# Nyström attention and a squared-ReLU FFN on one core: token-major A for two batches, landmark sums by adding transfers, and a new order

## The chip, the cores and the metric

The kernel runs on one core of one Trainium2 chip. A core has five engines that each work through their own instructions in order: TensorE (PE for its matmuls, PEld for its weight loads), VectorE (DVE), ScalarE (ACT), GpSimd (POOL) and SyncE (SP). They meet only through semaphores. Transfers are issued by POOL (the software queue, which also casts f32 to bf16 on the way) and by SP (the stores), and are carried out by 16 DMA engines. The metric is the time of one execution on the device in microseconds, as the median of several runs.

## The reference, cut to what matters

Eight batches of eight heads; 576 tokens, 64 columns per head, 32 landmarks per head. Each landmark is the mean of 18 neighbouring tokens. The attention output, laid out as 4608 tokens of 512 columns, goes through a feed-forward network with a squared ReLU.

```python
scale = 1.0 / np.sqrt(D)
q_lm = q.reshape(B, H, m, S // m, D).mean(axis=3)
k_lm = k.reshape(B, H, m, S // m, D).mean(axis=3)
A  = sm(q, k_lm)        # softmax of scale * a @ b^T
Bm = sm(q_lm, k_lm)
C  = sm(q_lm, k)
Z = Bm^T / (norm1(Bm) * norminf(Bm) + 1e-06)
for _ in range(6):
    Z = 2 * Z - Z @ Bm @ Z
attn = A @ Z @ C @ v
x = attn.transpose(0, 2, 1, 3).reshape(B * S, H * D)
h = x @ w_in            # 512 -> 2048
r = np.maximum(h, 0.0)
out = (r * r) @ w_out   # 2048 -> 512
```

## The kernel before

**Who sets the order.** The kernel is written as a list of operations, each with a name, the engines that could do it, a cost on each, what it reads and writes, and the PSUM banks that it takes. A planner (class `Plan`) runs through them once while the kernel is built: at each moment each free engine takes, of its ready operations, the one with the largest tail (the length of work behind it, plus a bias from the table `URGE`); an operation that two engines could do goes to the one that would end first (table `LEAN` shifts that). The result is a fixed order on each engine, emitted as it is. The due times of the planner are its own; on the chip an instruction waits for what it needs, and everything behind it on its engine waits too.

**Stages of one batch b.** Names in the list are those of the operations.

- Loads: `ldk`, `ldq` (L480, two transfers of 590 KB each into tile X), `ldv` (L489, tile V), w_in in eight transfers, w_out in four, all on POOL. At most eight of these transfers are in flight; POOL waits for a free place before it issues the next. Before the change, the order is k and q of batch 0 in turn (k, q, k, q), v of batch 0, k and q of batch 1, w_in, v of batch 1, w_out, and then batch after batch.
- Landmark sums `lm`: PE adds 18 tokens by multiplying X with an identity. Batch 0 is done in two halves. Its first half and the whole of batch 1 are 18 full-array matmuls each (L535, "flat"); its second half and the other batches are 36 matmuls each that use PE as four arrays of 64x64 (L542) and leave two parts in two banks, which `lmc` (two copies) and `lme` (one addition) bring together into LM. The sums are not divided by 18; the scale of the mean is put into the exponentials.
- `lmt` and `T` (L519) transpose LM and X on DVE into LT and TT.
- `B` (L585): the 32x32 scores of landmarks against landmarks, then a softmax in small DVE steps (L601 writes Bf) and the start of Z. L631 is the matmul that adds B's columns.
- Z iterations: six times `N` (L694, PE) and `U` (L708, DVE), for batches 0 to 2 as small matmuls of 32x32, for the others as block-diagonal ones, whose operand BD is built by `bd` (L648).
- `SC`, `SA` or, for merged batches, `SS`: the scores of C (L730) and A (L725). C: maximum (L769), its negative scaled (`Cng`, L772), exponential with row sum (L775), reciprocal, scaling (`Cnr`), transpose `CT`. `CV` (L798) multiplies C with V.
- `Zm` (L817, four small DVE instructions) spreads Z into a block form, `ZC` (L824) multiplies it with CV, `W` (L842) multiplies the result with w_in into WP, evicted by `We` (L467 on ACT, L471 on DVE). So attention and the first FFN matrix are joined: FFN1 is A times WP.
- A: DVE transposes the scores from PSUM (`At`, L882), then maximum, subtraction (L889), exponential on ACT (L891), sum, scaling (L899) and a transpose `Ab` (L902) into AT.
- FFN1 `F` (L928): PE, weights WP, moving AT; ReLU `R` on ACT (L945) or DVE (L947) into RS; square `Q` on DVE (L956) or ACT (L954) into G. Batches 0 and 1 do this in two parts of 320 and 256 tokens, the others in one of 576.
- FFN2 `O` (L974): 36 output tiles of 128 tokens, 16 matmuls each; eviction `Oe`, store `St` (SP).

FFN1 of batch b and FFN2 of batch b-1 are woven together on PE, and the attention of the batches ahead is put between them. Until the first `O`, matmuls on constant data fill PE's gaps (L1086).

The softmax of C, and the spreading of Z, as they are before:

```python
op(f"Cng{b}.{r}", {"DVE": 0.1}, ...)                    # -SCALE/SEG * max
op(f"Cex{b}.{r}", {"ACT": a_(576) + 0.27}, lambda e, r=r: nc.scalar.activation(
    Cs[r][:].rearrange("p x u -> p u x"), cbanks(r),
    AF.Exp, bias=s_[:, 12 + r:13 + r], scale=SCALE / SEG,
```

Of the kernel before, what the change touches and what calls it, by code (L numbers as in the profile page):

```python
# [8 lines left out]
P = 128  # L9
# [20 lines left out]
RING = 2 * S  # L30

# [23 lines left out]
class Plan:  # L55
# [14 lines left out]
    def op(self, name, engs, emit, R=(), W=(), alloc=(), nbytes=0, queue=None, after=(), bias=0.0,  # L70
           crit=False, port=(), mode="full", ni=8):
# [6 lines left out]
        o.uses = [x for x in {id(x): x for x in [*R, *W] if isinstance(x, Bank)}.values()]  # L78
# [52 lines left out]
    def schedule(self, limits):  # L131
# [6 lines left out]
        free = {e: 0.0 for e in ENGINES}  # L138
        queues = {"sw": 1.5, "hw": 0.0}
# [7 lines left out]
        events, done, t, count = [], 0, 0.0, 0  # L147
# [9 lines left out]
        def banks_for(xs):  # L157

            got, taken = [], {}
            for x in xs:  # L160
# [7 lines left out]
                for i in range(0, 9 - x.n, 2 if x.n == 2 else 1):  # L168
# [6 lines left out]
                    if x.n == 2 or owner[i ^ 1] is not None:  # L175
                        best = i
                        break
# [8 lines left out]
        while done < len(self.ops):  # L186
            moved = True
            while moved:
                moved = False
                for e in ENGINES:  # L190
# [53 lines left out]
                    elif o.nbytes:  # L244
                        q = o.queue
                        queues[q] = max(queues[q], free[e] + 0.5) + o.nbytes / RATE[q]
                        o.end = queues[q] + 1.7
# [62 lines left out]
RATE = {"sw": 0.405e6, "hw": 0.2e6}  # L310
# [53 lines left out]
def kernel(  # L364
# [35 lines left out]
    AT = [mk(f"AT{i}", [P, 2, S], BF16) for i in range(3)]  # L400
# [4 lines left out]
    ZC = [mk(f"ZC{i}", [P, 4, M], BF16) for i in range(2)]  # L405
# [8 lines left out]
    Bt = [mk(f"Bt{i}", [P, 2, M], BF16) for i in range(2)]  # L414
    sm = [mk(f"sm{i}", [P, 18], F32) for i in range(2)]
# [11 lines left out]
    msel = mk("msel", [P, 4], F32)  # L427
    blkb = mk("blkb", [P, 4, M], BF16)
# [24 lines left out]
    def c_blk(e):  # L453
# [3 lines left out]
        blk2[:], blkb[:, 0:2], blkb[:, 2:4], ALU.add), R=["blkb"], W=["blk2"])  # L457
    op("c7", {"ACT": 0.2}, lambda e: nc.scalar.activation(warm[:], onesf[:, 0:1], AF.Exp),
       R=["onesf"], W=["warm"])

# [21 lines left out]

    def load_v(b):
# [10 lines left out]
    def load_win(z, r, hf):  # L494
        src = moe_w_in[:, 1024 * hf:1024 * hf + 1024].rearrange("(h d) f -> d h f", d=D)
        op(f"win{hf}{z}{r}", {"POOL": 0.57},
           lambda e: nc.gpsimd.dma_start(
               w_in[64 * r:64 * r + 64, 2 * z:2 * z + 2, 1024 * hf:1024 * hf + 1024],
               src[:, 4 * r + 2 * z:4 * r + 2 * z + 2, :]),
           W=[("win", z, r, hf)], nbytes=524288, queue="sw")  # L500
# [8 lines left out]
    def attention(b):  # L509
# [5 lines left out]

# [9 lines left out]


        def landmarks(rs):
# [4 lines left out]
            def lmx(e):  # L532
# [13 lines left out]
               {"PE": 18 * max(n * 0.000424, 0.102) + 0.03 if flat else pe(n, 9) + 0.05}, lmx,  # L546
# [3 lines left out]
            if flat:  # L550
                op(f"lme{b}.{rs[0]}", {"ACT": 0.1 + ap_(n), "DVE": v_(n)},
                   lambda e: copy(e, o, view(bank(pl_))), R=[pl_], W=kL)
                return
            ls, kS = LS[i2][:, rs[0]], ("LS", i2, rs[0])
            for h in range(2):
                op(f"lmc{b}.{rs[0]}{h}", {"ACT": 0.17 + 0.00083 * n, "DVE": v_(n)},
                   lambda e, h=h: copy(e, ls[64 * h:64 * h + 64, 0:n],
                                       bank(pl_, 1)[64 - 64 * h:128 - 64 * h, 0:n]),
                   R=[pl_], W=[(kS, h)])
            op(f"lme{b}.{rs[0]}", {"DVE": v_(n)}, lambda e: nc.vector.tensor_tensor(  # L560
                o, view(bank(pl_)), view(ls), ALU.add), R=[pl_, (kS, 0), (kS, 1)], W=kL)

        rss = ((0,), (1,)) if b in SPLIT_LM else ((0, 1),)
        for rs in rss:
            landmarks(rs)
# [15 lines left out]
        def sB(e):  # L581
# [6 lines left out]
        op(f"B{b}", {"PE": 0.14}, sB, R=[kLT(0), kLT(1)], W=[pB], alloc=[pB], mode="32x32", ni=32)  # L588
# [7 lines left out]
            bl[:], bl[:], AF.Exp, scale=SCALE / (SEG * SEG)), R=[kb("bl")], W=[kb("bl")])  # L596
        op(f"Bsu{b}", {"DVE": 0.135}, lambda e: nc.vector.tensor_reduce(
            s_[:, 2:4], bl[:], axis=AX.X, op=ALU.add), R=[kb("bl")], W=[kb("bsu")])
        op(f"Brc{b}", {"DVE": 0.09}, lambda e: nc.vector.reciprocal(s_[:, 4:6], s_[:, 2:4]),
# [40 lines left out]
        op(f"Bad{b}", {"DVE": 0.08}, lambda e: nc.vector.tensor_scalar(  # L640
            out=s_[:, 8:10], in0=s_[:, 6:8], scalar1=1e-6, scalar2=None, op0=ALU.add),
           R=[kb("n1")], W=[kb("n2")])
        op(f"Brn{b}", {"DVE": 0.13}, lambda e: nc.vector.reciprocal(s_[:, 10:12], s_[:, 8:10]),
           R=[kb("n2")], W=[kb("rn")])
        pY = Bank(1, "att")

        whole = b not in TILED
        bdiag = lambda e, o, i: eng(e).tensor_tensor(  # L648
# [15 lines left out]
        o_bbt = op(f"BBT{b}", {"PE": 0.15}, bbt,  # L664
# [12 lines left out]
        for it in range(6):  # L677
# [23 lines left out]
            op(f"N{b}.{it}", {"PE": 0.15 if whole else 0.1}, nm,  # L701
# [41 lines left out]
        def sCA(e, i):  # L743
            u = i ^ int(pSs[0].at > pSs[1].at)
            for w in range(2):
                for r in range(2):
                    for c in range(4):
                        mmC(c, r, w, u, pSs[i].at + r)
                        mmA(c, r, w, i)

        def cbanks(r):
            if not merged:
                return pair(pSs[r], HALF)
            lo, hi = sorted(x.at for x in pSs)
            return ps[:, lo + r:hi + r + 1:hi - lo, 0:HALF]

        kA = lambda t: [kLT(0), kLT(1), kt(t, 0), kt(t, 1)]
        if merged:
            for i in range(2):
                op(f"SS{b}.{i}", {"PE": 0.3}, lambda e, i=i: sCA(e, i),  # L760
                   R=[*kA(0), *kA(1)], W=[pSs[i], pAs[i]], alloc=[pSs[i], pAs[i]], mode="32x32", ni=64)
        else:
            for rs in rss:
                op(f"SC{b}.{rs[0]}", {"PE": pe(HALF, 4) + 0.03}, lambda e, rs=rs: sC(e, rs),
                   R=[x for r in rs for x in (kLT(r), kt(1, r))], W=[pSs[r] for r in rs],
                   alloc=[pSs[r] for r in rs], mode="32x32", ni=32 * len(rs))
        for r in range(2):
            R = [*pSs] if merged else [pSs[r]]
# [408 lines left out]
```

## Time and profile before

| What | Value |
|---|---|
| Median of 3 runs | 270.96 us (270.51 to 271.35) |
| Span of the profiled execution | 269.5 us |
| PE busy | 250.8 us (93%) |
| PEld busy | 136.9 us (51%) |
| DVE busy | 210.6 us (78%) |
| ACT busy | 181.1 us (67%) |
| POOL busy | 48.7 us (18%) |
| Read from memory | 36.70 MB |
| Written | 9.44 MB |

The profile follows one execution. Its page gives the busy time of each engine, then the span in 40 slices (one digit is the busy share in tenths), the transfers, and the chain that ended last: from the last instruction back to what released it, step by step. A line of a group reads: source line, engine, operation, output <- input with partitions x elements and type, count, then busy time in us and the mean of one in ns, then idle time ahead of it and what ended most of that. The granted clock of PE is at full speed in every slice. The time around the span (270.96 against 269.5 us) belongs to no engine.

The windows further down give, for one stretch of time, the busy time of each engine in it. A group of matmuls shows busy times that overlap, since they are pipelined.

### The profile page before, as it was taken

Reading aid. Unit: us, or ns where it says so; the run is one execution under the profiler, and the core shown is the slowest. Engines: PE = TensorE matmul, PEld = TensorE weight load, DVE = VectorE, ACT = ScalarE, POOL = GpSimd, SP = SyncE. Lnnn points to the kernel's source line nnn. Section 1 sums busy time; section 2 is a strip of 40 time slices with the busy share of each in tenths; the row PEclk is TensorE's granted clock in tenths of the full one; section 3 lists DMA queues with packets and bytes.
Section 4 is the critical chain, followed back from the end, with each engine's and each line's share of the span. In section 5 each row is a group of like instructions: output and inputs, shape, how many; then the busy total and the mean of one; then the engine's idle time right before and its main releaser. Section 6 shows DMA issues by size and latency. Waiting matters only on the chain.

```text
span 269.5 us, 7826 instructions
## 1 busy us (share of the span) xinstructions
PE 250.8 (93%) x3170; PEld 136.9 (51%) x3170; DVE 210.6 (78%) x596; ACT 181.1 (67%) x372; POOL 48.7 (18%) x89
## 2 busy tenths in 40 slices
PE   5878898999969999999999999999999999999993
PEld 1534344545534446654555546645555555466452
DVE  2699899999969899789995799967997999265100
ACT  2043898899955699667887559866666679486310
POOL 8443523434310400200001013300000200000000
PEclk9999999999999999999999999999999999999999
DMA  6999999999992983451118031031103111321133
GB/s 105 207 195 203 207 206 211 210 243 216 221 223 43 151 150 83 71 118 44 34 43 168 2 78 43 2 78 41 39 2 76 46 41 40 74 47 39 39 80 78
DMA packets 16260, 28.30 MB, mean 105 GB/s; under 512 B 2272, under 2 KB 4576, under 8 KB 16224
## 3 DMA queue, kind: packets, MB, share of 16 engines
q0 software_dynamic: 10304, 18.35, 38.7%
q1 hardware_dynamic: 5840, 9.38, 14.0%
q8 instruction: 25, 0.41, 0.6%
q14 instruction: 11, 0.09, 0.1%
q10 hardware_dynamic: 80, 0.07, 0.1%
HBM read 36.70 MB, written 9.44 MB: 171 GB/s over the span
## 4 chain that ended last, share of the span: by engine, by line
PE 61%; DVE 16%; DMA 10%; ACT 9%; issue 2%; POOL 0%; DVEq 0%; POOLq 0%
PE ps L974 34%; PE ps L928 17%; DMA w_in<-in_moe_w_in_dram 4%; DMA X<-in_q_dram 4%; ACT C L775 3%; DMA X<-in_k_dram 2%; PE ps L842 2%; ACT RS L945 2%; PE ps L542 2%; PE ps L798 2%; DVE G L956 2%; DVE sm L769 2%; DVE RS L947 1%; DVE SA L882 1%; DVE smA L885 1%
## 5 line engine op out<-in xcount | busy, mean ns | idle before, releaser
L974 PE MATMUL ps<-w_out,G 128*128 128x512 bf16 (+1 forms) x592 | 140.3, 374 | 0.8 <-DVE sm L769 0.7
L945 ACT ACTIVATE RS<-ps 128x576 bf16<-128x576 f32 (+2 forms) x150 | 76.3, 558 | 18.1 <-PE ps L928 13.8
L928 PE MATMUL ps<-AT,WP 128*128 128x288 bf16 (+2 forms) x512 | 77.7, 286 | 3.5 <-ACT RS L945 2.0
L974 PEld LDWEIGHTS <-G 128*128 128x128 bf16 x592 | 53.7, 98 | 52.1 <-issue 5.7
L928 PEld LDWEIGHTS <-WP 128*128 128x128 bf16 x512 | 47.8, 97 | 30.2 <-issue 7.8
L956 DVE TENSOR_TENSOR G<-RS 128x576 bf16<-128x576 bf16 (+2 forms) x96 | 38.7, 413 | 11.1 <-ACT RS L945 9.7
L467 ACT COPY OS<-ps 128x512 f32<-128x512 f32 (+2 forms) x33 | 18.9, 574 | 23.7 <-PE ps L974 16.8
L954 ACT ACTIVATE G<-RS 128x256 bf16<-128x256 bf16 (+2 forms) x64 | 32.8, 549 | 2.1 <-DVE RS L947 1.6
L519 DVE STREAM_TRANSPOSE TT<-X 128x576 uint32<-128x576 uint32 x32 | 23.9, 757 | 5.8 <-DMA X<-in_k_dram 4.9
L467 ACT CAST WP<-ps 128x1024 bf16<-128x1024 f32 x22 | 21.8, 1014 | 4.9 <-PE ps L842 4.6
L648 POOL TENSOR_TENSOR BD<-ST,blkb 128x256 bf16<-128x256 bf16 x13 | 9.6, 737 | 80.1 <-DVE ST L708 68.4
L489 POOL DMA_DIRECT2D V<-in_v_dram x24 | 12.5, 529 | 32.5 <-PE ps L798 18.6
L775 ACT ACTIVATE C<-ps,sm 128x576 bf16<-128x576 f32 x16 | 14.2, 908 | 6.0 <-DVE sm L772 5.2
L471 DVE CAST WP<-ps 128x1024 bf16<-128x1024 f32 x10 | 12.1, 1212 | 5.8 <-PE ps L842 4.8
L708 DVE SCALAR_TENSOR_TENSOR ST<-ST,ps 128x128 bf16<-128x128 bf16 (+1 forms) x48 | 12.5, 261 | 4.5 <-PE ps L694 3.1
L471 DVE COPY OS<-ps 128x512 f32<-128x512 f32 (+1 forms) x5 | 3.0, 606 | 14.7 <-ACT OS L467 14.7
L891 ACT ACTIVATE SA<-SA 128x640 f32<-128x640 f32 (+1 forms) x16 | 11.1, 693 | 4.9 <-DVE SA L889 4.9
L882 DVE STREAM_TRANSPOSE SA<-ps 128x320 f32<-128x320 f32 (+1 forms) x32 | 13.4, 459 | 0.7 <-PE ps L725 0.5
L769 DVE TENSOR_REDUCE sm<-ps 128x1 f32<-128x576 f32 x16 | 11.5, 744 | 2.0 <-ACT SA L891 1.7
L842 PE MATMUL ps<-w_in,ZC 64*32 64x512 bf16 x256 | 11.1, 382 | 1.7 <-DMA w_in<-in_moe_w_in_dram 0.7
L899 DVE TENSOR_TENSOR An<-SA,smA 128x640 bf16<-128x640 f32 (+1 forms) x16 | 12.6, 794 | 0.0
L480 POOL DMA_DIRECT2D X<-in_q_dram x16 | 8.5, 534 | 21.8 <-DVE Bf L601 6.7
(91 smaller groups left out, 260.7 us busy)
## 6 DMA issues: line engine op xcount, KB each, us to landing
out_dram<-OS SPq DMA_DIRECT2D x70, 128.0 KB, 2.4
X<-in_k_dram POOLq DMA_DIRECT2D x16, 288.0 KB, 10.0
X<-in_q_dram POOLq DMA_DIRECT2D x16, 288.0 KB, 10.3
V<-in_v_dram POOLq DMA_DIRECT2D x8, 288.0 KB, 9.2
w_in<-in_moe_w_in_dram POOLq DMA_DIRECT2D x8, 256.0 KB, 11.1
w_out<-in_moe_w_out_dram POOLq DMA_DIRECT2D x4, 512.0 KB, 12.0
V<-in_v_dram POOLq DMA_DIRECT2D x8, 216.0 KB, 9.2
V<-in_v_dram POOLq DMA_DIRECT2D x8, 72.0 KB, 8.7
```

Source lines behind the costliest of these rows:

```text
L467: nc.scalar.copy(o, i)
L471: eng(e).tensor_copy(o, i)
L519: op(f"T{b}.{t}{r}", {"DVE": v_(576)}, lambda e, r=r: nc.vector.transpose(tt[:, t, r].rearrange("p s m e -> p (s m e)").bitcast(U32), x[:, ...
L769: op(f"Cmx{b}.{r}", {"DVE": v_(576)}, lambda e, r=r: nc.vector.tensor_reduce(s_[:, 12 + r:13 + r], cbanks(r), axis=AX.XY, op=ALU.max), R=R ...
L775: op(f"Cex{b}.{r}", {"ACT": a_(576) + 0.27}, lambda e, r=r: nc.scalar.activation(Cs[r][:].rearrange("p x u -> p u x"), cbanks(r), AF.Exp, ...
L842: nc.tensor.matmul(ps[quad(pos_a(c, r)), pW.at + r, :], lhsT=ZC[i2][half, pos_c(c, r), :], rhs=w_in[half, c, 512 * ch:512 * ch + 512], sta ...
L882: nc.vector.transpose(sa[:, z].rearrange("p s m -> p (s m)"), ps[:, pS.at + z, 0:M * n])
L928: nc.tensor.matmul(ps[:, ph.at + i, 0:w], lhsT=wp[:, r, 128 * f:128 * f + 128], rhs=at[:, r, lo + w * i:lo + w * i + w], start=(r == 0), s ...
L945: nc.scalar.activation(o, x, AF.Relu)
L954: nc.scalar.activation(o, x, AF.Square)
L956: nc.vector.tensor_tensor(o, x, x, ALU.mult)
L974: nc.tensor.matmul(bank(po)[:, 0:c1 - c0], lhsT=G[:, f, lo:lo + P], rhs=w_out[:, f, c0:c1], start=(f == 0), stop=(f == NF - 1))
```

## The change

- **Landmark sums of batches 3 to 7** (`ADDED`) leave PE. For each of these batches POOL issues 18 more transfers of 131 KB (nine for k, nine for q). Each takes two of the 18 tokens of every landmark, straight from the inputs, into one f32 accumulator tile LD; the first of the nine writes, the others add to what is there. Then one addition (`lmc`) joins the two halves and one scaled copy (`lme`) writes LM.
- **Token-major A for batches 0 and 1** (`TOKENS`). The scores of A come out with tokens on the partitions: 20 full-array matmuls per batch (`SA`) with TT as weights and a block form BK of the landmark keys (`bk`, DVE or POOL) as the moving side. The softmax works from PSUM; the first two transposes of DVE fall away. 10 matmuls with an identity (`Ap`) turn the result, and `Ab` becomes a copy from PSUM, on ACT or DVE. The two parts of FFN1 are then 256 and 320 tokens.
- **Z doubled and scaled at once** for batches 0 to 2 (`DUP`). C is no longer divided by its row sums; the reciprocals go through a small matmul (`CR`) into CRS, and one matmul pair (`Zd`) copies Z to both halves of the partitions, so that one DVE instruction (`Zm`) spreads and scales it. `Cnr` and the four `Zm` fall away there.
- **Scales**: the mean's scale is put into the landmarks (`LMS`), so the exponentials of A and C need none; `Cng` falls away, as the maximum is taken negated.
- **C's banks side by side**: both banks of one half of C are neighbours in every batch; in merged batches (now 2 to 7) both pairs are taken by the first `SS`.
- **Order and plan**: w_in is loaded in chunks of 512 columns; the loads follow the list `LOAD_ORDER`; FFN1 of batch 0 runs in blocks of eight (`F_BLOCK`); the first group of an output tile stands behind FFN1 of its batch; ZC is two tiles; the planner's costs and its tables `URGE` and `LEAN` are new (the tables hold some 500 numbers and are left out below), so the order of almost all instructions is a new one.

Per kernel this is, by instructions: 252 to 72 at L542; 256 to 192 matmuls of A in the old form, 40 new of `SA`, 20 of `Ap`, 6 of `CR`, 6 of `Zd`; squares on ACT 64 to 27, on DVE 96 to 133; transfers issued by POOL 68 to 158.

```diff
+LMS = SCALE / SEG
+    LD = {b: mk(f"LD{b}", [P, 2, 2, 2, D], F32) for b in ADDED}
...
+    def add_landmarks(b):
+        for s in range(SEG // 2):
+            for t in range(2):
+                src = (q, k)[t][b].rearrange("(r c) (m s) d -> (c m) r (s d)", r=2, s=SEG)
+                kd = ("LD", b, t)
+
+                def add(e, s=s, t=t, src=src):
+                    nc.gpsimd.dma_start(LD[b][:, t].rearrange("p r j d -> p r (j d)"),
+                                        src[:, :, 128 * s:128 * s + 128],
+                                        **({"accum_op": ALU.add} if s else {}))
+                op(f"la{b}.{s}{t}", {"POOL": 0.6}, add, R=[kd] if s else [], W=[kd],
+                   nbytes=131072, queue="sw")
...
+        def landmarks_added():
+            ls = LS[i2].rearrange("p r n -> p (r n)")[:, 0:256].rearrange("p (t r d) -> p t r d", t=2, d=D)
+            op(f"lmc{b}.0", {"DVE": v_(256), "POOL": g_(256)}, lambda e: eng(e).tensor_tensor(
+                ls, LD[b][:, :, :, 0], LD[b][:, :, :, 1], ALU.add),
+               R=[("LD", b, 0), ("LD", b, 1)], W=[("LS", i2, 0)], port=("POOL", "DVE"))
+            op(f"lme{b}.0", {"ACT": 0.36, "DVE": 0.25}, lambda e: copy(e, lm[:], ls, scale=LMS),
+               R=[("LS", i2, 0)], W=[("LM", i2, r) for r in range(2)])
...
-            landmarks(rs)
+            if b in ADDED:
+                landmarks_added()
+            else:
+                landmarks(rs)
...
             op(f"Cmx{b}.{r}", {"DVE": v_(576)}, lambda e, r=r: nc.vector.tensor_reduce(
-                s_[:, 12 + r:13 + r], cbanks(r), axis=AX.XY, op=ALU.max),
+                s_[:, 12 + r:13 + r], cbanks(r), axis=AX.XY, op=ALU.max, negate=True),
                R=R, W=[kb(f"cmx{r}")])
-            op(f"Cng{b}.{r}", {"DVE": 0.1}, lambda e, r=r: nc.vector.tensor_scalar(
...
+            def cr(e):
+                for r in range(2):
+                    nc.tensor.matmul(bank(pR)[:, 0:8], lhsT=cpick[:, r].rearrange("p z r m -> p (z r m)"),
+                                     rhs=cmx_[:, r].rearrange("p q r -> p (q r)"),
+                                     start=(r == 0), stop=(r == 1))
...
+            def zd(e):
+                for h in range(2):
+                    nc.tensor.matmul(
+                        bank(pD)[:, 64 * h:64 * h + 64].rearrange("p (j m) -> p j m", j=2),
+                        lhsT=dupm[:, h].rearrange("p z x -> p (z x)"),
+                        rhs=zt[:, :, 1, :], start=True, stop=True)
+            op(f"Zm{b}", {"DVE": v_(256)}, lambda e: nc.vector.tensor_tensor(
+                zm[:], bank(pD)[:, 0:P].rearrange("p (q m) -> p q m", q=4)
+                .unsqueeze(2).to_broadcast([P, 4, 2, M]),
+                crs[:].unsqueeze(3).to_broadcast([P, 4, 2, M]), ALU.mult),
+               R=[pD, kb("crs")], W=[(*kzm, i) for i in range(4)])
...
+            def tm(e, u=u, pS=pS):
+                for r in range(2):
+                    for g in range(2):
+                        for w in range(2):
+                            s0, j = 8 * u + 4 * g, 2 * r + g
+                            nc.tensor.matmul(bank(pS)[:, P * j:P * j + P],
+                                             lhsT=tt[:, 0, r, s0:s0 + 4, :, w],
+                                             rhs=BK[:, r].rearrange("p c (m w) -> p c m w", w=2)[:, :, :, w],
+                                             start=(w == 0), stop=(w == 1))
...
+            def tr(e, u=u, pT=pT, anv=anv):
...
+                        nc.tensor.matmul(ps[:, at, c0:c0 + 128].rearrange("p (s m e) -> p s m e", e=2, m=M),
+                                         lhsT=f(2 * r + g), rhs=turn,
+                                         start=True, stop=True)
...
+            op(f"Ab{b}.{u}", {"DVE": v_(128 * n), "ACT": ap_(128 * n)}, lambda e, u=u, pT=pT, t0=t0, n=n: copy(
+                e, at_part(b, t0, t0 + 64 * n),
+                pair(pT, 320) if u else bank(pT).rearrange("p (r n) -> p r n", r=2)),
+               R=[pT], W=[("AT", b % 3, u)])
...
+                                     after=f1_ops[bl][-4:-3] if g == 0 and bl else ()))
...
+F_BLOCK = {0: 8}
+LOAD_ORDER = [
+    "ldk0", "ldq0", "ldv0", "win1", "win0", "ldq1", "ldk1", "win2", "win3", "la3", "wout0",
+    "wout1", "wout2", "la4", "wout3", "ldv1", "ldq2", "ldk2", "ldv3", "ldk4", "ldv2", "ldk3",
+    "ldq4", "ldq3", "ldv4", "la5", "ldk5", "ldq5", "ldv5", "la6", "ldk6", "ldq6", "ldv6", "la7",
+    "ldk7", "ldq7", "ldv7"
+]
+DUP = (0, 1, 2)
+TOKENS = (0, 1)
+ADDED = (3, 4, 5, 6, 7)
-MERGED = (1, 2, 3, 4, 5, 6, 7)
+MERGED = (2, 3, 4, 5, 6, 7)
```

More of the change, by code (lines that the diff above doesn't have):

```diff
@@ L70, in op @@
     def op(self, name, engs, emit, R=(), W=(), alloc=(), nbytes=0, queue=None, after=(), bias=0.0,
[L71 removed]
+           crit=False, port=(), mode="full", ni=8, holds=()):
         o = Op()
@@ L146, in schedule @@
         held = {}
-        events, done, t, count = [], 0, 0.0, 0
+        events = [(T0[e], -1 - i, None) for i, e in enumerate(ENGINES)]
+        heapq.heapify(events)
+        done, t, count = 0, 0.0, 0
         def push(o):
@@ L167, in banks_for @@
                 best = None
-                for i in range(0, 9 - x.n, 2 if x.n == 2 else 1):
+                for i in range(0, 9 - x.n, 2 if x.n > 1 else 1):
                     mine = range(i, i + x.n)
@@ L308 @@
 ENGINES = ("PE", "ACT", "DVE", "POOL", "SP")
-RATE = {"sw": 0.405e6, "hw": 0.2e6}
+RATE = {"sw": 0.375e6, "hw": 0.2e6}
+T0 = {"PE": 1.1, "ACT": 1.1, "DVE": 1.1, "POOL": 1.31, "SP": 1.1}
+SW0, LAND = 1.5, 1.75
 def a_(n):
@@ L414 @@
     Bt = [mk(f"Bt{i}", [P, 2, M], BF16) for i in range(2)]
+    CMX = [mk(f"CMX{i}", [P, 2, 4, 2], F32) for i in range(2)]
+    CRS = [mk(f"CRS{i}", [P, 4, 2], F32) for i in range(2)]
     sm = [mk(f"sm{i}", [P, 18], F32) for i in range(2)]
@@ L869, in attention @@
+        for u in () if b in TOKENS else range(2):
             pS = pAs[u]
@@ L1018, in weave, with loads @@
         return [o for _, _, o in sorted(keyed, key=lambda z: z[:2])]
-    def loads(what, b=0):
+    def loads(what, b):
         if what == "kq":
@@ L1029, in loads @@
             load_v(b)
+        elif what == "la":
+            add_landmarks(b)
         elif what == "win":
             for r in range(2):
-                for z in range(2):
-                    load_win(z, r, b)
-        else:
-            for i in range(4):
-                load_wout(i)
+                load_win(r, b)
+        else:
+            load_wout(b)
     rank = []
```

241 lines of the change are left out of this document (172 added, 69 removed), and 96 rows, old and new, of tables (LEAN, URGE).

## The prediction

> **What bounds the kernel now.** I read the 40 slices of the page first, then ten-microsecond windows, then the chain of waits, then single groups. The profiled execution has a span of 269.5 us; the median of the runs is 270.96 us, so 1.5 us lie around the span and are added at the end.
>
> The windows (columns: stretch, then busy time of PE, PEld, DVE, ACT and POOL, the granted clock, DMA share, GB/s):
>
> ```profile
> 30.00:40.00 10.00, 8.79 (x135) 4.31 (x130) 8.55 (x29) 8.95 (x24) 3.57 (x7) 1.00 1.22 205
> 40.00:50.00 10.00, 8.96 (x149) 4.88 (x147) 9.63 (x27) 9.33 (x28) 2.93 (x6) 1.00 1.14 211
> ...
> 60.00:70.00 10.00, 9.78 (x175) 5.53 (x173) 9.56 (x30) 9.95 (x31) 3.69 (x7) 1.00 1.11 221
> 70.00:80.00 10.00, 7.92 (x121) 4.28 (x119) 8.04 (x30) 7.49 (x23) 2.62 (x4) 1.00 1.11 222
> ...
> 130.00:140.00 10.00, 10.00 (x83) 5.83 (x88) 9.93 (x25) 8.71 (x15) 0.29 (x1) 1.00 0.12 27
> ```
>
> Three stages show. After 90 us PE never rests and what it has to do is the time. From 30 to 90 us DVE and ACT are as full as PE. The DMA engines are full until 80 us and nearly idle behind it.
>
> The chain of waits (start, length, what) gives the first stage and the pieces of PE work in question:
>
> ```profile
> 2.56 6.41 DMA X<-in_k_dram
> ...
> 9.26 10.20 DMA X<-in_q_dram
> ...
> 19.74 11.05 DMA w_in<-in_moe_w_in_dram
> ...
> 51.14 1.14 PE ps L542 x36
> ...
> 61.05 1.11 PE ps L542 x36
> ...
> 147.22 3.10 PE ps L542 x108
> ...
> 249.58 15.59 PE ps L974 x88
> ```
>
> Until 30 us the chain is loads. L542 is a landmark sum of one batch: 36 matmuls, about 1.1 us; three stand in one piece at 147 us, while PE is the bound. The last piece is the tail at full pace: 0.213 us for a 128x512 matmul. Measured against that pace, the starts of all matmuls of L928 and L974 between 30 and 90 us lose 9.4 us; after 100 us they lose about 0.3 us in ten.
>
> The groups that price the rest (count | busy us, mean ns):
>
> ```profile
> L954 ACT ACTIVATE G<-RS 128x256 bf16<-128x256 bf16 (+2 forms) x64 | 32.8, 549 | 2.1 <-DVE RS L947 1.6
> ...
> L882 DVE STREAM_TRANSPOSE SA<-ps 128x320 f32<-128x320 f32 (+1 forms) x32 | 13.4, 459 | 0.7 <-PE ps L725 0.5
> ...
> L817 DVE TENSOR_TENSOR ZM<-ST,blk 64x128 bf16<-64x128 bf16 x32 | 7.0, 218 | 0.4
> ...
> L535 PE MATMUL ps<-X,ident 128*128 128x128 bf16 x18 | 2.1, 308 | 2.1 <-DMA X<-in_q_dram 2.1
> ```
>
> **The change, part by part.**
>
> *Start, until the first matmul of L928 (now at 28.26 us).* k and q of batch 0 are now loaded k, k, q, q, so the first landmark group needs the third transfer instead of the second. DVE starts on these transfers at 7.11 (second) and 8.99 us (third): the first group of 18 runs 9.0 to 11.1 us, the second, now right behind it, to 11.8 instead of 11.2. Token-major A puts 20 matmuls between L631 and the first Z iteration; at 2.08 us for 18 such matmuls (7.22 us, L535) they take 2.3 us where L725 took 0.70, and delay the first iteration (17.17 us) by about 1 us. The other way, the landmark sum of batch 1 (2.12 us at 19.54) no longer cuts the iterations apart: those around it stand 2.5 us apart, the others 0.95, so 1.6 us come back, and one 128x256 product (about 0.42 us, by L471 CAST LM) replaces four of L817 (0.93 us). So ZC stays at about 25.5 us (now 25.14). But the sum of batch 1 now stands between ZC and the first W in PE's order. It needs k and q of batch 1, queued behind 2.1 MB more of w_in: 8.0 MB of source in all, which today has landed at 25.6 us. Then 2.1 us: W at 27.9 instead of 26.37; eviction 1.01 us; and B of batch 1, which also stands ahead, waits for DVE's row to about 29.2. First FFN1 matmul 29.5 us: +1.2 us. Bounds: 0 (if ZC is ahead of X) and +3 (if both chains add).
>
> *Landmark sums of batches 3 to 7.* Gone from PE: 1.11, 1.12 (in the window 70 to 80) and 3.10 us, together -5.3 us, four fifths of it in or next to the stage where PE is the bound. Their DVE and ACT work (two copies of 0.42 and an addition of 0.42) becomes one addition and one copy, half of it.
>
> *What they cost instead.* 90 transfers of 131 KB, 11.8 MB beside the 36.7 MB of source now loaded. POOL issues one X transfer in 0.55 us: 90 x 0.55 = 50 us more on 48.7, spread over 140 us, so POOL itself is not full. Two of one accumulator stand eight or so transfers apart in POOL's order, as far as its queue makes any two of them wait today, so no new wait appears at issue until the last pair of batch 3. The queue lands 204 GB/s in slices 2 to 6 as bf16, so 0.41 MB/us of source: 0.32 us for a plain 131 KB. No row shows an adding transfer. From below, 0.32 us each; from above, the lone small V transfer late in the run, 4.4 us from issue to landing, if nothing overlapped. I take 1.3 times plain, near the lower end, because eight are always in flight. What is late next if it is more is the first rival. At my price the ninth pair of batches 3, 5 and 6 (31.4, 44.8 and 47.8 MB down the queue) lands at 84, 120 and 129 us; PE gets to the B matmuls of these batches at about 90, 133 and 142 us, and 2 us lie between (addition, scaling, transpose). Cost 0, covered by 4 to 11 us.
>
> The Trainium skill (DMA: Bandwidth & Descriptors, Rules for kernel authors) states that an accumulating transfer reads its destination and writes it later. No run here shows it; if reading both sides doubled the price, the sum below would lose its gain, as the first rival works out from rows.
>
> *Token-major A, batch 1, and the rest of batch 0.* On PE behind the first FFN1 matmul: 20 + 16 full-array matmuls at 0.11 = +3.9 us, less 32 of L725 (0.5 us), plus two small products per batch for Z (0.5 us): +3.9. If only their 128 columns counted (half of a 256-column matmul, 2.12 us / 18 / 2 = 0.06): +2.2. I take +3.4, near the row that has the same form.
>
> *DVE and ACT from 30 to 90 us.* Batch 1 drops four transposes of L882 (1.84 us) and two of L902 (0.92) from DVE and gives two copies (about 1.3 us) to ACT. 23 squares of batches 0 and 1 move from ACT (437 and 502 ns) to DVE (280 and 311 ns): -10.6 on ACT, +6.7 on DVE. Batches 1 and 2 lose L772, L817 and the scaling of C, 2.1 us each, against 0.8 for what replaces it: -2.6. Together about 8 us of two engines that are both full, 4 us of time, taken from the 9.4 that the FFN matmuls lose there. Bounds: 0 (the relief lies where neither is last) and -9.4 (all of it). I take -4.
>
> *New order of loads, banks of C side by side, scales folded in.* The order is in the first item; w_out lands about 2 us earlier (33.9 for 36.0), which PE doesn't wait for. C's banks add no instruction; L772 (138 ns, 16 of them) goes from a DVE that is full: counted above for two batches, hidden behind PE afterwards.
>
> Sum: +1.2 - 5.3 + 0 + 3.4 - 4 = -4.7, and 0.7 for the five returns from the 64x64 mode around L542 (61.05 + 1.11 to 62.30 shows 0.14 each): -5.4. Span 264.1, time about **265.6 us**. The item bounds run from -16 to +6 around it; they don't all fall on one side, so its own range is 260 to 270.
>
> **The rivals.**
>
> *Adding transfers too dear (slower).* Mechanism: PE works in order; B of batch 6 stands ahead of FFN matmuls and waits for the last pair of its accumulator. 74 adding transfers lie ahead of that point. At twice plain they add 74 x 0.32 = 24 us to 121.5 (plain): landing 145.5; PE is there at 142 and 2 us lie between, so 5.5 us of stall, time 271. At 2.5 it is 157 and 17 us of stall: 283 us. It decides from about twice plain. For: the transfers are the only thing in the change that no row prices, and the queue is already full for 80 us. Against: eight are in flight, and the bytes are small. In the middle of the two it is 276. 21 of 100.
>
> *The relief is not where the wait ends.* DVE carries 6.7 us more squares; if DVE is what FFN1 of batches 0 and 1 waits for, the 9.4 us stay. Then -5.3 + 3.4 + 1.2 - 0.7 = -1.4: 269.6 us. For: DVE is at 9.63 and 9.56 of 10. Against: ACT is at 9.95 beside it. 14 of 100.
>
> *All of the stall goes.* With both engines below 90% PE runs at tail pace from 30 us on: -9.4 instead of -4, 260.2 us. For: the window 130 to 140 shows PE full with DVE at 9.93. Against: order on PE is fixed and B and N matmuls wait there for chains. 9 of 100.
>
> *The forecast:* 56 of 100.
>
> **How the numbers follow.** A measurement of this kernel tells about 0.3% (0.8 us) from no change. Faster by more: 0.54 of the forecast's 0.56, the third rival (0.09) and two thirds of the second (0.09): 0.72. Within: most of the rest of the second and a little of the first, 0.06. Slower: most of the first rival (0.19) and the tails of the others (0.03): 0.22. The range reaches down past the third rival to 259 and up into the first one, 273, which leaves its dearer half (0.13) and the low tail (0.05) out.
>
> **What would show it.** Right: no matmul on X after 70 us; first FFN1 matmul at 29 to 30 us; the FFN matmuls of 30 to 90 us losing about 5 us; seven output tiles begun by 85 us; DMA share high until 125 us. Wrong: PE waiting at B of batch 3, 5 or 6 for an LD transfer; adding transfers landing more than 0.6 us apart with the queue full; an earlier or later first FFN1 by more than 2 us.

## The result and the profile after

The changed kernel takes 302.19 us (301.32 to 303.33), the kernel before 270.77 us: 1.117 times as long (95% interval 1.114 to 1.121). Forecast was 265.6 us with a range of 259 to 273; the change is slower, on the side of the first rival, and further than its price. Some executions took over 1.5% longer than the fastest of their kernel; medians and ratios in this text leave these out.

The page of the changed kernel: the span; of part 1 the engines; of part 2 POOL, the granted clock of PE and the DMA share; of part 3 POOL's queue (packets, MB, share of 16 engines); of part 5 the adding transfers.

```profile
span 301.6 us, 7543 instructions
...
PE 262.2 (87%) x3003; PEld 141.1 (47%) x3003; DVE 211.4 (70%) x607; ACT 170.4 (56%) x343; POOL 151.1 (50%) x172
...
POOL 8445779689779969899989674110000000000000
PEclk9797999999799788997985968999999999999999
DMA  6999999999999999999997965301311312012242
...
q0 software_dynamic: 33568, 30.16, 65.0%
...
L527 POOL DMA_DIRECT2D LD<-in_k_dram x45 | 83.0, 2132 | 4.4 <-DMA LD<-in_k_dram 3.4
L527 POOL DMA_DIRECT2D LD<-in_q_dram x45 | 78.6, 1859 | 9.7 <-DMA LD<-in_q_dram 5.4
```

POOL's busy time has gone from 48.7 to 151.1 us, the DMA engines are full until about 160 us and busy until 180 (80 before), and the granted clock, which was full in all 40 slices, falls again and again until 183 us. The windows that were shown of before (the columns are the same) tell where:

```profile
30.00:40.00 10.00, 9.52 (x102) 5.99 (x101) 9.22 (x32) 9.00 (x25) 7.11 (x9) 1.00 1.23 220
40.00:50.00 10.00, 9.90 (x172) 5.83 (x173) 7.95 (x23) 8.10 (x22) 9.29 (x11) 1.00 1.26 197
...
60.00:70.00 10.00, 10.00 (x130) 5.83 (x129) 9.37 (x46) 8.86 (x29) 8.54 (x11) 1.00 1.22 199
70.00:80.00 10.00, 8.03 (x98) 3.20 (x68) 6.18 (x13) 3.23 (x7) 9.28 (x11) 0.87 1.22 204
...
130.00:140.00 10.00, 7.38 (x103) 3.31 (x101) 7.19 (x20) 5.00 (x11) 10.00 (x12) 0.83 1.30 207
```

From 30 to 70 us PE is busier than before (9.5 to 10.0 against 8.8 to 9.8): this fits the forecast relief of DVE and ACT. From 70 us on PE, DVE and ACT all rest while POOL is full. The chain of waits names what they rest for (start, length, what):

```profile
93.71 4.78 POOL LD L527 x4
98.48 11.00 DMA LD<-in_k_dram
...
109.57 0.43 DVE LS L578
...
111.42 0.24 PE ps L757 x2
```

POOL is busy with issues into LD, the transfer that it issues at 98.48 us lands 11 us later, DVE adds the two halves of the landmarks, and only then PE goes on. The addition behind the last pair (L578) starts at 100.1, 109.6, 157.8, 178.5 and 188.0 us for batches 3 to 7; the prediction had the pairs of batches 3, 5 and 6 land at 84, 120 and 129. The waits on PE (line, waited for: us in total, times, longest):

```profile
PE ps L757 <- DVE BD L711: 10.0, 2, 7.6
PE ps L646 <- DVE sm L701: 6.4, 1, 6.4
PE ps L646 <- DVE LT L630: 3.5, 1, 3.5
PE ps L721 <- POOL BD L711: 2.6, 1, 2.6
```

L646 is the matmul of the landmark scores, L757 a Z iteration of another batch whose operand stands behind the waiting copy of the landmarks on DVE. And most of these waits are paid twice. Windows of two microseconds around the longest one:

```profile
152.00:154.00 2.00, 0.62 (x5) 0.25 (x3) 0.00 (x0) 0.65 (x1) 2.00 (x4) 1.00 1.06 170
154.00:156.00 2.00, 0.00 (x0) 0.00 (x0) 0.00 (x0) 0.00 (x0) 1.95 (x2) 0.97 1.40 177
156.00:158.00 2.00, 0.00 (x0) 0.00 (x0) 0.00 (x0) 0.00 (x0) 0.92 (x2) 0.50 1.36 168
...
162.00:164.00 2.00, 2.00 (x16) 1.00 (x15) 1.34 (x4) 0.65 (x1) 2.00 (x5) 0.50 0.79 96
164.00:166.00 2.00, 2.00 (x24) 0.86 (x24) 1.50 (x5) 0.65 (x1) 2.00 (x5) 0.50 1.01 122
166.00:168.00 2.00, 2.00 (x21) 0.87 (x26) 1.72 (x7) 0.78 (x3) 2.00 (x5) 0.97 0.98 123
```

PE stops at 152.6, the granted clock (the column behind POOL) falls to 0.50 about 3.3 us later, and stays there until 166 us, 6 us after PE has work again at 160.2. A wait of 2.0 us is enough to stand ahead of such a fall (it ends at 77.1):

```profile
76.00:78.00 2.00, 0.90 (x10) 0.38 (x10) 1.19 (x3) 1.90 (x5) 2.00 (x3) 0.85 1.13 213
78.00:80.00 2.00, 2.00 (x6) 0.76 (x5) 2.00 (x7) 0.94 (x2) 1.28 (x3) 0.50 1.22 187
```

After 70 us seven waits of PE last 2.0 to 7.6 us, and behind six of them the clock is at 0.50 for 3.4 to 10.2 us; behind the one that ends at 86.3 (2.1 us) it stays full. Two more falls, at 9.1 and 22.8 us, lie before 30 us.

### The profile page after: what moved, and what is told of

Read it like the earlier page. It is cut to its first block, busy times and chain, and to the rows that moved or that the text cites. A ratio compares the mean times of both kernels' runs of the same rounds, so it can differ in the third digit from the quotient of the medians.

```text
span 301.6 us, 7543 instructions
## 1 busy us (share of the span) xinstructions
PE 262.2 (87%) x3003; PEld 141.1 (47%) x3003; DVE 211.4 (70%) x607; ACT 170.4 (56%) x343; POOL 151.1 (50%) x172
## 3 DMA queue, kind: packets, MB, share of 16 engines
q0 software_dynamic: 33568, 30.16, 65.0%
## 4 chain that ended last, share of the span: by engine, by line
PE 40%; DMA 31%; POOL 20%; DVE 4%; issue 3%; ACT 0%; POOLq 0%; DVEq 0%
PE ps L1140 25%; POOL LD L527 15%; PE ps L1094 11%; DMA w_in<-in_moe_w_in_dram 7%; DMA X<-in_k_dram 5%; DMA LD<-in_k_dram 5%; DMA w_out<-in_moe_w_out_dram 4%; DMA LD<-in_q_dram 3%; DMA V<-in_v_dram 3%; DMA X<-in_q_dram 3%; POOL X L517 3%; POOL V L539 1%; PE ps L938 1%; PE ps L879 1%; PE ps L793 1%
## 5 line engine op out<-in xcount | busy, mean ns | idle before, releaser
L1111 ACT ACTIVATE RS<-ps 128x576 bf16<-128x576 f32 (+2 forms) x152 | 77.6, 568 | 33.4 <-PE ps L1094 22.8
L527 POOL DMA_DIRECT2D LD<-in_k_dram x45 | 83.0, 2132 | 4.4 <-DMA LD<-in_k_dram 3.4
L527 POOL DMA_DIRECT2D LD<-in_q_dram x45 | 78.6, 1859 | 9.7 <-DMA LD<-in_q_dram 5.4
L1122 DVE TENSOR_TENSOR G<-RS 128x576 bf16<-128x576 bf16 (+2 forms) x133 | 51.6, 396 | 13.0 <-ACT RS L1111 11.6
L539 POOL DMA_DIRECT2D V<-in_v_dram x24 | 24.1, 1356 | 7.1 <-DMA w_out<-in_moe_w_out_dram 2.9
L517 POOL DMA_DIRECT2D X<-in_q_dram x16 | 19.2, 1244 | 2.0 <-DMA V<-in_v_dram 1.0
L517 POOL DMA_DIRECT2D X<-in_k_dram x16 | 15.2, 971 | 5.5 <-DMA X<-in_k_dram 1.7
L757 PE MATMUL ps<-ST,BD 128*128 128x64 bf16 (+1 forms) x60 | 6.7, 194 | 10.0 <-DVE BD L711 10.0
L1120 ACT ACTIVATE G<-RS 128x576 bf16<-128x576 bf16 (+2 forms) x27 | 14.1, 554 | 0.2
L757 PEld LDWEIGHTS <-BD 128*128 128x128 bf16 x60 | 5.4, 100 | 15.2 <-DVE BD L711 11.5
L1258 PE MATMUL ps<-onesb 128*128 128x512 bf16 x31 | 10.9, 485 | 1.5 <-DVE onesb L449 1.5
```

Of the source, the lines that this page charges most:

```text
L517: lambda e: nc.gpsimd.dma_start(x[:, t, r].rearrange("p s d -> p (s d)"), src),
L527: nc.gpsimd.dma_start(LD[b][:, t].rearrange("p r j d -> p r (j d)"), src[:, :, 128 * s:128 * s + 128], **({"accum_op": ALU.add} if s else {}))
L539: lambda e, r=r, p0=p0, n=n, src=src: nc.gpsimd.dma_start(vv[32 * p0:32 * (p0 + n), r].rearrange("p s d -> p (s d)"), src),
L1111: nc.scalar.activation(o, x, AF.Relu)
L1120: nc.scalar.activation(o, x, AF.Square)
L1122: nc.vector.tensor_tensor(o, x, x, ALU.mult)
```

## The experiments

All comparisons are with the kernel before on the same chip (270.7 to 271.0 us in each set).

**1. The same order, the 80 adding transfers plain.** Each accumulator keeps only its last pair of tokens; the sums are left out.

```diff
-                                        **({"accum_op": ALU.add} if s else {}))
```

> The changed kernel with the same order, in which the 80 adding transfers write plainly (each accumulator keeps only its last pair of tokens; the sums are left out). Theory A, adding is what costs: in the changed kernel's own trace the first, plain transfer of an accumulator lands 0.35 us behind the one ahead of it and an adding one 0.72, and POOL needs 0.73 against 1.2 us to issue one. Then the landings here are 0.35 us apart, POOL's busy time falls from 151 to about 110 us (80 x 0.47 less, and fewer waits), the stalls of 2 to 7.6 us on PE after 70 us go, the granted clock is above 0.97 and the time is 263 to 270 us. Rival B, the number of small transfers is what costs, adding or not: landings 0.7 us apart, 295 us or more. Rival C, the order of loads in one queue is what costs (transfers stand behind X tiles that are still being read): POOL's waits for landed transfers stay, and the time is above 285 us.

Measured: 278.5 us median; 1.027 times before (1.021 to 1.033). The page's line of POOL's queue, and the durations of the transfers into LD (ns: least, median, most):

```profile
q0 software_dynamic: 15648, 30.16, 51.7%
...
L527 POOL DMA_DIRECT2D LD<-in_q_dram x45: 702/722/760, 21.2 to 157.8; - x45
L527 POOL DMA_DIRECT2D LD<-in_k_dram x45: 707/722/770, 22.6 to 159.9; - x45
```

The same 30.16 MB in less than half the packets: 33568 - 15648 = 17920, 224 more for each of the 80 adding transfers. In a full queue four in a row land at 90.42, 90.80, 91.17 and 91.55 us, 0.38 apart; four adding ones in the changed kernel land at 108.69, 109.48, 110.20 and 110.90, 0.74 apart. POOL's busy time is 110.1 us. Adding alone costs 302.2 - 278.5 = 23.7 us: theory A in the price, but not in the sum: the time is 8.5 us above its upper bound of 270, and one wait of 7.0 us on PE is left. Three lines of this trace (of an execution of 281.7 us) show where it comes from, a wait of DVE, and on POOL the issue that the addition stands behind:

```profile
DVE LM L510 <- POOL LS L577: 7.3, 1, 7.3
...
140.71 0.72 POOL L527 DMA_DIRECT2D LD<-in_q_dram  x1 [4.70 <-issue]
141.45 0.73 POOL L577 TENSOR_TENSOR LS<-LD 128x256 f32<-128x256 f32 x1
```

The addition of batch 5 is an instruction of POOL. DVE waits from 134.9 us. Until 139.65 the last pair of batch 5 has not landed, although it is written plainly; that is the larger part. After that the addition stands behind a transfer into the accumulator of batch 7 until 141.45, another 1.8 us. This transfer waits 4.70 us: until 138.56 for the landing of the one before it into the same bytes, and 2.1 us more for which the trace names no cause. So rival C holds in part: an accumulator is a chain, and POOL's queue is in order. In the changed kernel the same wait of DVE (7.9 us) is almost all landing: the last pair of batch 5 comes at 157.28, the addition starts at 157.83.

**2. The price by itself.** Twenty transfers behind the last load of the kernel before.

```diff
+        for tiles, w in ((small, 128), (large, 256)):
+            for plain in (True, False):
+                for i, x in enumerate(tiles):
...
+                    nc.gpsimd.dma_start(x[:], src[:, :, 0:w], **({} if plain else {"accum_op": ALU.add}))
```

> The kernel before, with 20 extra transfers into spare tiles behind the last load on POOL (about 230 us on, the queue otherwise empty): six plain of 131 KB in pieces of 512 bytes, six adding of the same, four plain of 262 KB in pieces of 1024 bytes, four adding. The output is unchanged. Theory A, an adding transfer is dear by its bytes: adding 512 B lands every 0.72 us, adding 1024 B every 1.4, plain 0.35 and 0.64. Rival, dear by its pieces (each read and written once): adding 1024 B lands every 0.8 to 1.0 us. If POOL's issue is the limit, landings stand 1.2 us apart for both adding sizes and 0.73 for both plain ones.

POOL's timeline (start, length, what), in turn: six plain of 131 KB, six adding, four plain of 262 KB, four adding.

```profile
214.73 4.38 POOL L1099 DMA_DIRECT2D XS<-in_k_dram  x6
220.59 7.41 POOL L1099 DMA_DIRECT2D XS<-in_k_dram  x6 [1.48 <-DMA XS<-in_k_dram]
225.01 5.93 POOL L1099 DMA_DIRECT2D XL<-in_k_dram  x4
233.33 4.99 POOL L1099 DMA_DIRECT2D XL<-in_k_dram  x4 [2.39 <-issue]
```

An issue takes POOL 4.38 / 6 = 0.73 us plain, 7.41 / 6 = 1.24 adding, and 4.99 / 4 = 1.25 for an adding one of twice the bytes (the third row starts while POOL is still behind with the second, so its length says nothing). The landings stand 0.40 us apart for 131 KB plain (220.04 to 222.04), 1.16 adding (224.82 to 230.60, near POOL's own 1.24), 1.06 for 262 KB plain (232.08 to 235.26) and 2.09 adding (238.67 to 244.94). So in the queue an adding transfer costs about twice a plain one (2.09 against 1.06, where POOL is not the limit); on POOL it costs about 1.25 us at both sizes.

**3. The rest of the change without adding transfers.**

```diff
-ADDED = (3, 4, 5, 6, 7)
+ADDED = ()
```

> The changed kernel without its adding transfers (ADDED empty): batches 3 to 7 get their landmark sums from PE again, everything else of the change is kept, and the planner's tables are fitted anew, since the old ones leave the planner stuck. Theory A (adding transfers and what stands behind them in POOL's queue are all of the loss): 266 to 272 us, no PE wait above 2 us after 70 us, granted clock above 0.98. Rival: the rest of the change (token-major A, doubled Z, load order) is itself slow, as the 278.5 us of the run with plain transfers could also mean: 275 us or more, with waits on PE between 70 and 160 us.

Measured: 269.1 us (0.994 of before, 0.992 to 0.997), no PE wait above 1.0 us after 10 us, granted clock 0.975 to 0.993 (above 0.98 was expected). By time and waits theory A holds. Without the transfers the change is worth a little, not the 5.4 us of the forecast; PE has its landmark sums back, and the order is another one.

**4. Adding transfers for the last two batches alone.** `ADDED = (6, 7)`, the planner's price of one set to 1.2 us on POOL and 0.75 us in the queue.

> As the run without adding transfers, but with them for batches 6 and 7 alone, planned with 1.2 us on POOL and 0.75 us in the queue for each. Theory A: 36 transfers (32 adding) fit behind the loads, where the queue of the kernel before is nearly empty, and PE loses two sums of 1.1 us with their returns from 64x64 mode: 1 to 3 us below the run without any, 264 to 270 us. Rival: POOL's queue is in order and any accumulator stalls what stands behind it: PE waits of more than 3 us at the landmark scores of batches 5 to 7, slower than the run without any.

Measured: 1.000 of before (0.996 to 1.004), ten executions from 268.8 to 276.2 us. Neither side is shown: in the profiled execution, one of the fastest (269.25 us), PE has no wait above 1.3 us after 10 us, so no accumulator stalls what stands behind it there; but there is no gain over experiment 3 (0.994) either.

**5. PE kept busy ahead of the first landmark sum.** Five more fillers (128x512 matmuls on ones) in experiment 3.

> As the run without adding transfers, with five more filler matmuls right ahead of the first landmark sum, where PE sat idle for 2.4 us in the changed kernel and the granted clock then fell to 0.50 for about 4 us. If idle time on PE is what lowers the clock, the granted clock stays at 1.00 from 8 to 16 us, and the first FFN1 matmul and the end come 0.5 to 2 us earlier. If the clock falls for another reason (the product work in the array, a shared limit), it falls here too and the time is that of the run without.

Measured: 269.3 us against 269.1. PE is busy for 1.74 instead of 0.13 us in 6 to 8, and that won nothing. Without it, PE of experiment 3 sat idle for 3.1 us there, longer than in the changed kernel (2.4), and the clock stayed full. It fell later in both, at 24.9 us in experiment 3 (for 3.4 us) and at 19.1 in experiment 5 (for 10.2 us; two of its windows):

```profile
18.00:20.00 2.00, 1.56 (x85) 1.19 (x82) 1.99 (x6) 0.74 (x1) 1.19 (x2) 0.79 1.11 210
20.00:22.00 2.00, 1.13 (x46) 0.63 (x31) 1.74 (x5) 0.65 (x2) 0.79 (x2) 0.50 1.11 210
```

PE is busy for three quarters of the first window, with Z iterations of 32x32 and the small matmuls of CV, and the clock still falls. In experiment 3 PE does much the same work in that window, and it does not fall. So a wait of 2 us or more stands ahead of each fall of the changed kernel after 70 us, but not ahead of every fall, and the clock does not fall behind every wait. What sets it off is left open.

**6. Also without token-major A.** `ADDED = ()`, `TOKENS = ()`.

> The change without adding transfers and without token-major A (TOKENS empty), tables fitted anew. If token-major A pays as the prediction had it (3.4 us more on PE, about 4 us of two full engines relieved between 30 and 90 us), this is within 2 us of the run with it. If it costs more than it gives, this is 2 us or more faster.

Measured: 265.0 us, 0.980 of before (0.977 to 0.982). Faster by 4.1 us than with it: it costs more than it gives. Much of it is the start: the first FFN1 matmul stands at 27.88 us here, at 31.05 in experiment 3, 3.2 us later.

**7. All 90 transfers, planned with the measured price.** The planner's cost of an adding transfer is corrected; `URGE` and `LEAN` together hold two entries here, where the runs with fitted tables have some 470 to 520.

```diff
-                op(f"la{b}.{s}{t}", {"POOL": 0.6}, add, R=[kd] if s else [], W=[kd],
-                   nbytes=131072, queue="sw")
+                op(f"la{b}.{s}{t}", {"POOL": 1.2 if s else 0.73}, add, R=[kd] if s else [], W=[kd],
+                   nbytes=280000 if s else 131072, queue="sw")
```

> The whole change, all 90 transfers kept, with the planner told what the traces show of an adding transfer (1.2 us on POOL, 0.75 us in the queue) and its tables fitted to that. Theory A, the price itself is the loss: 80 x 0.72 + 10 x 0.35 = 61 us of queue behind and between 90 us of loads cannot be hidden wherever they stand, and the time stays 8 us or more above the run without adding transfers (269.1): 277 to 295 us. Rival: the loss came of an order that was laid out for cheap transfers, and an order that knows the price hides them: 272 us or less.

Measured: 282.0 us (two executions, 280.8 and 283.1; 1.042 of before, 1.035 to 1.048). An order that knows the price wins back 20 us of the 33 between 302.2 and 269.1; 13 stay. That lies within theory A's bounds, but with two entries the order is close to unfitted, not fitted as the expectation has it. How much of the 13 us a fitted order would hide is not shown.

**8. Wide pieces.** Six tokens to a transfer, 30 transfers of the same bytes in all, two accumulators that batches take in turn.

```diff
-        for s in range(SEG // 2):
+        for s in range(SEG // 6):
...
-                                        src[:, :, 128 * s:128 * s + 128],
+                                        src[:, :, 384 * s:384 * s + 384],
...
+            op(f"lmc{b}.0", {"DVE": v_(1536)}, lambda e: nc.vector.tensor_reduce(
+                ls, LD[b].rearrange("p t r j d -> p t r d j"), axis=AX.X, op=ALU.add),
```

> As the run with the measured price, but each transfer carries six tokens of every landmark in pieces of 1536 bytes instead of two in 512: 30 transfers of 393 KB instead of 90 of 131 KB, the same bytes, 20 adding instead of 80; DVE adds the six partial sums (about 1.7 us per batch more). If POOL's 1.2 us per issue and the waits between transfers of one accumulator are what binds, POOL's busy time falls by about 70 us and the time is 5 us or more below that run. If the queue binds, by bytes as the price run showed (about 2 us per 262 KB adding), 20 x 2.2 + 10 x 1.0 = 54 us of queue stand against 61, and the time is within 4 us of that run.

Measured: 272.8 us, 1.008 of before (1.006 to 1.011): 9 us below experiment 7 and 3.7 above experiment 3, which has no adding transfers. POOL's busy time fell by 148.7 - 74.9 = 73.8 us. The bytes are the same and two thirds of them are added instead of eight ninths, which at the landings' price is worth 7 us of queue (61 - 54). The 9 us meet the condition set for POOL and the waits (5 us or more), but the tables of this run are fitted and those of experiment 7 are not, so how they split between the queue, POOL, the shorter chains and the order is not shown. One line shows what it costs on DVE:

```profile
L579 DVE TENSOR_REDUCE LS<-LD x5: 2778/2817/2834, 64.1 to 164.3; 128x256 f32<-128x1536 f32 x5
```

2.8 us for a sum over six, 1.1 more than the 1.7 expected.

**9. A second fit of experiment 6.**

> The change without adding transfers and without token-major A, with tables from a longer fit of the planner than in the run before (its own end is 1.1 us earlier). Both kernels should be beaten: 263 to 266 us. If two fits of one set of options differ by more than 3 us on the chip, the 4.1 us between the runs with and without token-major A say nothing.

Measured: 266.0 us (0.983, 0.980 to 0.987), 1.0 us above the first fit. So these two fits differ by 1 us, and the 4.1 us of token-major A (3.1 by this fit) are more than that, though not known to the microsecond.

**10. Also without the doubled Z.** `ADDED`, `TOKENS` and `DUP` empty.

> Without adding transfers, without token-major A and without the doubled Z (DUP empty); what is left of the change are the scales, the banks of C, the order of the loads and the fitted order. If the doubled Z takes 2.6 us of DVE work out of two batches at a time when DVE is full, as the prediction had it, this is 1 to 4 us slower than the run with it (265.0). If it hides behind other work, within 1 us.

Measured: 269.5 us (0.995, 0.992 to 0.997): 3.5 to 4.5 us slower than experiments 9 and 6. The doubled Z pays, at the upper end of what was expected. But the first FFN1 matmul moves from 27.2 or 27.9 to 32.8 us, by more than the whole loss, so the run does not show that the gain is DVE work saved at a time when DVE is full.

**11. The changed kernel's own order with the adding transfers left out.** Each accumulator holds its first pair; the sums are left out.

```diff
                 def add(e, s=s, t=t, src=src):
+                    if s:
+                        return
```

> The changed kernel with its own order, in which the 80 adding transfers are not issued at all (each accumulator holds its first pair of tokens; the sums are left out). Theory A, the 80 transfers are the whole loss: without them the forecast's other terms are left, 261 to 268 us (the prediction's sum of 265.6 had them at no cost), and the steps are 302 (adding), 278.5 (plain), about 265 (none). Rival: the rest of the change in this order loses by itself (a late start, a lower clock in the first 30 us, token-major A): 270 us or more.

Measured: 264.5 us (0.977, 0.975 to 0.980). The page and two windows, from the stretches where the changed kernel stood still:

```profile
span 262.8 us, 7412 instructions
...
PE 245.5 (93%) x2962; PEld 136.3 (52%) x3003; DVE 210.8 (80%) x607; ACT 170.2 (65%) x343; POOL 51.5 (20%) x92
```

```profile
70.00:80.00 10.00, 9.79 (x165) 4.97 (x165) 10.00 (x24) 4.76 (x10) 3.12 (x6) 1.00 1.03 214
...
150.00:160.00 10.00, 9.95 (x98) 5.94 (x98) 9.97 (x28) 8.56 (x16) 1.34 (x2) 1.00 0.23 52
```

The steps are 302.2 (adding), 278.5 (plain), 264.5 (none): 23.7 us for adding, 14.0 for the transfers themselves. The spans of the first and the last differ by 38.8 us. PE's gaps of half a microsecond and more sum to 31.7 us in the changed kernel and 6.2 here, 25.5 more. The clock is at 0.50 during eight stretches of the changed kernel, in which PE is busy for 28.9 us, and during one of experiment 11, with 2.8; at half speed about half of that is lost, 13 us more (an estimate; the busy times themselves, 262.2 and 245.5, can't be compared, as this trace has 2962 matmul records and the other 3003). 25.5 + 13 = 38.5 of 38.8: the loss is waiting, and a slow clock that mostly follows waiting.

**12. The best parts together.** No token-major A, doubled Z, wide adding transfers for batches 5 to 7.

> No token-major A, doubled Z kept, and adding transfers in the wide form (six tokens, pieces of 1536 bytes) for batches 5, 6 and 7 alone, planned with the measured price. PE loses three landmark sums (3.3 us and 0.14 for each return from 64x64 mode) against the run without adding transfers (265.0): 261 to 264 us if the 18 transfers hide behind 90 us, where the queue is nearly empty; 266 us or more if any accumulator is late for its scores.

Measured: 264.6 us (0.978, 0.976 to 0.981), within 0.4 us of experiment 6. The 18 transfers hide (no PE wait above 1.1 us behind the first matmul), but the 3.3 us of work that PE lost are not seen in the time; where they went is open. Experiments 6, 9 and 12 beat both kernels.

## Why the prediction was wrong

**The step that failed** is "What they cost instead", with its price of 1.3 times plain and its cost of 0. Four numbers of it were off. In the queue: 0.72 against 0.35 us in the same trace, 2.1 times plain. On POOL: 1.24 us per adding issue, where the prediction took the 0.55 of an X transfer and so 50 us instead of the 102 that were measured (151.1 - 48.7). The waits: "no new wait appears at issue until the last pair of batch 3" looked for two transfers of one accumulator too close in POOL's order, and left out that POOL falls behind the order: transfers into LD waited 10.0 us for earlier ones of their own in the changed kernel. And the additions of two batches are POOL's own instructions, which the prediction counted as DVE work: the one of batch 5 stands behind a waiting transfer of batch 7, for 1.8 us in experiment 1 and half a microsecond in the changed kernel.

The rule that stood beside it, from the Trainium skill (DMA: Bandwidth & Descriptors, Rules for kernel authors), that an accumulating transfer reads its destination and writes it later, fits the traces, which show about twice the price of a plain transfer, in the full queue and alone.

**The first rival** was what happened, and was too cheap: 271 us at twice plain, 283 at 2.5. It counted one stall, at batch 6. Batches 3 to 6 were all late, and it had neither POOL's 1.24 us nor the clock: at 0.50 for some microseconds behind most waits, worth about 13 us. The Trainium skill (TensorE: Matmul & The Clock Gate, What's actually happening) has the clock halve after an idle stretch of about 3.4 us and return after as much work; behind the 7.6 us wait the trace shows the fall 3.3 us after PE stopped, which agrees, and 6 us of work until the return, which is longer; and the clock fell behind waits of 2.0, 2.4 and 2.6 us too, which are shorter than the page's stretch.

**The other terms held in sum**, which experiment 11 shows, where only this one is taken out. Its time is 264.5 us; the sum was 265.6. Not every one held by itself.

- Start: first FFN1 matmul at 29.37 us there (29.5 predicted, 30.32 in the changed kernel, whose clock was 0.50 from 10 to 12 us).
- DVE and ACT from 30 to 90 us: the FFN matmuls lose 5.5 us against their pace, 9.4 before; -4 was predicted. What fell is ACT's busy time, 170.2 us over the whole span against 181.1 before; DVE's did not, 210.8 against 210.6. The prediction's own items say so too, if DVE's are added up by themselves (+6.7 - 1.84 - 0.92 - 2.6 = +1.3).
- Landmark sums gone from PE: experiment 3, with the sums back and another order, is 4.6 us above experiment 11; -6.0 was predicted with the mode returns.
- Token-major A: +3.4 us on PE against a share of 4 us of relief was taken as about even. With the order fitted anew, leaving it out wins 3 to 4 us, and the first FFN1 matmul comes 3 to 4 us earlier. So it gave less than counted, while the doubled Z, counted as 2.6 us of DVE work, gave 3.5 to 4.5 us of time. That the sum came out within 1.1 us is in part luck: errors of opposite sign met in it. In which stage either acts is not parted by these runs.
- The bounds: moving each item to its own bound gives about 8 us below the sum and 6 above, not 16 below.

## What to carry to other kernels

An adding transfer is not free work for an idle engine: here it costs the queue twice its bytes and POOL 1.24 us each, and each one waits for the one before into the same bytes, so that a late one makes the rest of its chain late. The forms that cost least here had few large pieces (experiment 8, close to before) or stood late, where the queue is nearly empty (experiment 12), and neither won anything over leaving them out. And price an operation that no row shows from its worst row when the forecast's whole gain hangs on it. A wait on PE can cost more than its length: behind six of seven waits of 2 us and more the clock was halved for 3.4 us or longer.

## What the runs showed of the hardware

POOL's time to issue an adding transfer does not grow with its size (1.24 us at 131 KB, 1.25 at 262 KB), while the distance of its landings does (1.16, near POOL's own pace, and 2.09 us; 0.74 for 131 KB in a full queue); an adding transfer of 131 KB has 224 more packets than a plain one. The granted clock fell to 0.50 at 19.1 us of experiment 5, in a window in which small matmuls kept PE busy for 1.56 of 2 us, and did not fall after one idle stretch of 3.1 us (experiment 3, 6 to 9 us); in the changed kernel it fell after one of 2.0 us.
